# Chunk sizes, half weight loads, one evacuating engine and split stores in a depthwise-separable 1x1 convolution

## The chip, the cores and the metric

The kernel runs on one core of a Trainium2 chip. The metric is the device time of one execution in microseconds (us), as the median of several runs. Profiles are of single executions; their own time stands beside their span.

## The reference

The input is one image of 384 x 384 positions with 384 channels, in bf16. The depthwise kernel is 1 x 1, so the depthwise step only scales each channel, and the pointwise step is a matrix product over channels:

```
for i in range(k):            # k = 1
    for j in range(k):
        out = out + xp[:, i:i+H, j:j+W, :] * dw[i, j][None, None, None, :]
return jnp.einsum('bhwc,cd->bhwd', out, pw)
```

So out[n, d] = sum over c of x[n, c] * dw[c] * pw[c, d], for N = 147,456 rows n and 384 values of c and of d.

## The kernel before

**Tiling.** The rows are cut into 288 supertiles of 512 rows. Supertiles are grouped into chunks, each loaded and stored by one DMA. `_chunks` gives the sizes: 1, 1, 2, 4, then 34 chunks of 8, then 4, 2, 1, 1. Three X buffers (`NX`) hold loaded chunks and three O buffers (`NO`) hold results; two T buffers and two PSUM halves (`PS`, four banks each) alternate by supertile.

**Weights.** `load_pw` loads pw four times, once into each quarter of 32 partitions, so that four row tiles of TensorE can work side by side. All four loads count on one semaphore, `s_pw`. The scales dw are spread by four VectorE copies into `dwsel` (L186). Then twelve slices of `w_r` (six blocks b, two parities) are made as pw times dw: the even parity on VectorE (L197), the odd on ScalarE (L199). Each adds to `s_wr`, and TensorE waits for all twelve before its loop starts.

**One supertile.** VectorE transposes X into T in two halves of 32 x 32 blocks of 32-bit words, that is of bf16 pairs (L174); half h serves blocks 3h to 3h + 2. TensorE (L134) then does 48 matmuls: twelve groups (b, parity) of four (q), where q picks one quarter of the array and one PSUM bank. It waits for the half of T it needs (`s_t`), and, in the first group, for the PSUM half to be empty (`s_a` from ScalarE, `s_d` from VectorE). When half h of the groups is through, `s_pe` rises. Banks 0 to 2 are then copied to O by ScalarE (L215), bank 3 by VectorE (L212).

**Order.** The order is written out by hand. VectorE runs, for supertile jj: the copy of bank 3, then the two transposes for jj + 2. ScalarE runs one copy per supertile. TensorE runs a hardware loop over pairs of supertiles. At the first supertile of a chunk, VectorE and ScalarE wait until the store of three chunks ago has landed (`s_o`), because it used the same O buffer. SP issues nearly all DMAs in program order: the first loads, then for each chunk t the load of chunk t + 3, which waits until chunk t has been transposed, and the store of chunk t, which waits for the last copies of the chunk. A waiting DMA holds back all that SP would issue after it.

In what follows the supertiles, chunks and stores are numbered from 0.

Of the kernel before, what the change touches and what calls it, by code (L numbers as in the profile page):

```python
# [7 lines left out]
BF16 = mybir.dt.bfloat16  # L8
F32 = mybir.dt.float32
U32 = mybir.dt.uint32  # L10
COPY = mybir.ActivationFunctionType.Copy
# [3 lines left out]
NO = 3  # L15


def _chunks(n_super: int):

    head, tail = [1, 1, 2, 4], [4, 2, 1, 1]  # L20
    mid = n_super - sum(head) - sum(tail)
    assert mid > 0 and mid % LMAX == 0
    return head + [LMAX] * (mid // LMAX) + tail
# [3 lines left out]
def kernel(  # L27
# [11 lines left out]
    nc = tc.nc  # L39
    P = nc.NUM_PARTITIONS  # L40
    B, H, W, C = x.shape
    assert dw.shape[0] == 1 and dw.shape[1] == 1, "only k=1 depthwise supported"
    D = pw.shape[1]
    N = B * H * W
    assert C == 384 and D == 384 and N % 1024 == 0
    NB = C // 64

    xf = x.rearrange("b h w c -> (b h w) c")
    of = out.rearrange("b h w d -> (b h w) d")

    NS = N // 512
    chunks = _chunks(NS)
    NT = len(chunks)
    s0 = [sum(chunks[:t]) for t in range(NT)]

    consts = ctx.enter_context(tc.tile_pool(name="consts", bufs=1))
# [3 lines left out]
    pw_r = consts.tile([P, NB, 2, D], BF16, name="pw_r")  # L60
    w_r = consts.tile([P, NB, 2, D], BF16, name="w_r")
    dwt = consts.tile([32, NB, 2], BF16, name="dwt")
    dwsel = consts.tile([P, NB * 2], F32, name="dwsel")
    warm = consts.tile([P, 3], F32, name="warm")
    seed = consts.tile([P, 2], F32, name="seed")

    Xs = [bufp.tile([P, 4 * LMAX, C], BF16, name=f"X{i}") for i in range(NX)]
    Ts = [bufp.tile([P, NB, 256], BF16, name=f"T{i}") for i in range(2)]
    Os = [bufp.tile([P, 4 * LMAX * D], BF16, name=f"O{i}") for i in range(NO)]
    PS = [psum.tile([P, 4, 512], F32, name=f"ps{s}") for s in range(2)]  # L70
# [2 lines left out]
    s_t = [[nc.alloc_semaphore(f"s_t{i}{h}") for h in range(2)] for i in range(2)]  # L73
    s_pe = nc.alloc_semaphore("s_pe")
    s_a = [nc.alloc_semaphore(f"s_a{i}") for i in range(2)]
    s_d = [nc.alloc_semaphore(f"s_d{i}") for i in range(2)]
    s_o = [nc.alloc_semaphore(f"s_o{i}") for i in range(NO)]
    s_dw = nc.alloc_semaphore("s_dw")
    s_pw = nc.alloc_semaphore("s_pw")
    s_ds = nc.alloc_semaphore("s_ds")  # L80
    s_wr = nc.alloc_semaphore("s_wr")
    s_seed = nc.alloc_semaphore("s_seed")

    with tc.tile_critical():  # L84
        pw_v = pw.rearrange("(b w r) d -> w b (r d)", w=32, r=2)
        dw_v = dw.rearrange("a e (b w r) -> w (a e b) r", w=32, r=2)

        def load_pw(eng, q):
            eng.dma_start(pw_r[32 * q : 32 * q + 32].rearrange("w b r d -> w b (r d)"), pw_v).then_inc(s_pw, 16)  # L89

        def load_x(t):
            L = chunks[t]
            r = 512 * s0[t]
            src = xf[r : r + 512 * L, :].rearrange("(p s) c -> p (s c)", p=P)
            d = nc.sync.dma_start(Xs[t % NX][:, : 4 * L, :].rearrange("p s c -> p (s c)"), src)  # L95
            if t >= NX:
                je = s0[t - NX] + chunks[t - NX] - 1
                d._wait_ge(s_t[je % 2][1], je // 2 + 1)
            d.then_inc(s_x[t % NX], 16)

        def store(t):
            L = chunks[t]
            r = 512 * s0[t]
            je = s0[t] + L - 1
            nc.sync.wait_ge(s_d[je % 2], je // 2 + 2)
            dst = of[r : r + 512 * L, :].rearrange("(q p j) d -> p q (j d)", q=4, p=P)
            d = nc.sync.dma_start(dst, Os[t % NO][:, : 4 * L * D].rearrange("p (q e) -> p q e", q=4))  # L107
            d._wait_ge(s_a[je % 2], je // 2 + 2)
            d.then_inc(s_o[t % NO], 16)


        nc.scalar.dma_start(dwt[:], dw_v).then_inc(s_dw, 16)
        load_x(0)
        load_pw(nc.scalar, 2)
        load_pw(nc.sync, 0)
        load_pw(nc.scalar, 3)
        load_pw(nc.sync, 1)
        for t in range(1, NX):
            load_x(t)
        for t in range(NT):  # L120
            if t + NX < NT:
                load_x(t + NX)
            store(t)
        for o in range(NO):
            nc.sync.wait_ge(s_o[o], 16 * len(range(o, NT, NO)))


        def supertile(s, rv):
            for b in range(NB):
                for par in range(2):  # L130
                    for q in range(4):
                        if par == 0 and q == 0 and b in (0, 3):
                            nc.tensor.wait_ge(s_t[s][b // 3], rv)
                        mm = nc.tensor.matmul(  # L134
                            PS[s][:, q, :D],
                            lhsT=Ts[s][32 * q : 32 * q + 32, b, par::2],
                            rhs=w_r[32 * q : 32 * q + 32, b, par, :],
                            start=(b == 0 and par == 0),
                            stop=(b == NB - 1 and par == 1),
                            tile_position=(32 * q, 0),  # L140
                        )
                        if b == 0 and par == 0 and q == 0:
                            mm._wait_ge(s_a[s], rv)
                        elif b == 0 and par == 0 and q == 3:
                            mm._wait_ge(s_d[s], rv)
                        if b in (2, 5) and par == 1 and q == 3:
                            mm.then_inc(s_pe)

        nc.tensor.wait_ge(s_wr, 2 * NB)
        with nc.tensor.Fori(0, NS // 2, 1) as it:  # L150
            rv = nc.tensor.to_reg(it + 1)
            for s in range(2):
                supertile(s, rv)


        for s in range(2):
            nc.vector.memset(seed[:, s : s + 1], 0.0).then_inc(s_d[s])  # L157
        nc.gpsimd.memset(warm[:], 0.0).then_inc(s_seed)  # L158
        for s in range(2):
            c = nc.scalar.copy(warm[:, s + 1 : s + 2], warm[:, 0:1])  # L160
            if s == 0:
                c._wait_ge(s_seed, 1)
            c.then_inc(s_a[s])

        def transposes(t, j):
            jj = s0[t] + j
            L = chunks[t]
            s = jj % 2
            Xw = Xs[t % NX][:].bitcast(U32)[:, : 4 * L, :].rearrange("p (k l) c -> p k l c", l=L)
            Tw = Ts[s][:].bitcast(U32).rearrange("p b (i k) -> p b k i", k=4)  # L170
            for h in range(2):
                if h == 0 and j == 0:
                    nc.vector.wait_ge(s_x[t % NX], 16 * (t // NX + 1))  # L173
                ins = nc.vector.transpose(  # L174
                    out=Tw[:, 3 * h : 3 * h + 3],
                    in_=Xw[:, :, j, 96 * h : 96 * h + 96].rearrange("p k (b w) -> p b k w", w=32),
                )
                if jj >= 2:
                    ins._wait_ge(s_pe, 2 * (jj - 2) + h + 1)
                ins.then_inc(s_t[s][h])  # L180

        order = [(t, j) for t in range(NT) for j in range(chunks[t])]

        nc.vector.wait_ge(s_dw, 16)
        for q in range(4):
            nc.vector.tensor_copy(  # L186
                dwsel[32 * q : 32 * q + 32, :], dwt[:].rearrange("w b r -> w (b r)")
            ).then_inc(s_ds)
        transposes(*order[0])
        for b in range(NB):  # L190
            for r in range(2):
                eng = nc.vector if r == 0 else nc.scalar
                if b == 0:
                    eng.wait_ge(s_pw, 64)  # L194
                sc = dwsel[:, 2 * b + r : 2 * b + r + 1]
                if r == 0:
                    i = nc.vector.tensor_scalar_mul(w_r[:, b, r, :], pw_r[:, b, r, :], sc)  # L197
                else:
                    i = nc.scalar.activation(w_r[:, b, r, :], pw_r[:, b, r, :], COPY, scale=sc)  # L199
                if b == 0:  # L200
                    i._wait_ge(s_ds, 4)
                i.then_inc(s_wr)
        transposes(*order[1])

        for jj, (t, j) in enumerate(order):
            L = chunks[t]
            s = jj % 2
            Ov = Os[t % NO][:, : 4 * L * D].rearrange("p (q j d) -> p q j d", q=4, d=D)
            if j == 0 and t >= NO:
                nc.vector.wait_ge(s_o[t % NO], 16 * (t // NO))  # L210
                nc.scalar.wait_ge(s_o[t % NO], 16 * (t // NO))  # L211
            e = nc.vector.tensor_copy(Ov[:, 3, j, :], PS[s][:, 3, :D])  # L212
            e._wait_ge(s_pe, 2 * jj + 2)
            e.then_inc(s_d[s])
            a = nc.scalar.copy(Ov[:, 0:3, j, :], PS[s][:, 0:3, :D])  # L215
            a._wait_ge(s_pe, 2 * jj + 2)
            a.then_inc(s_a[s])
            if jj + 2 < NS:
                transposes(*order[jj + 2])


# [28 lines left out]
```

## Time and profile before

| | |
|---|---|
| median of 9 runs | 586.66 us (585.78 to 589.11) |
| profiled execution | 586.6 us |
| its span | 584.8 us |
| TensorE matmul busy | 564.2 us (96%) |
| VectorE busy | 563.9 us (96%) |
| ScalarE busy | 327.0 us (56%) |
| moved by DMA | 227.79 MB, 390 GB/s over the span |

Busy time is the sum of the stretches in which an engine was at work. A matmul's busy time covers its wait in the pipeline, so a busy TensorE is not in itself a TensorE at its peak: the distance from one supertile's end to the next tells its pace. The chain that ended last is followed back from the end of the program, at each step to what released it; its entries are read as start, length, and what ran.

### The profile page before, as it was taken

The numbers are of one execution on the slowest core, as the hardware profiler recorded it, in microseconds if no ns is written. First come the engines' busy times: TensorE is split into PE (matmuls) and PEld (weight loads), VectorE is DVE, ScalarE is ACT, GpSimd is POOL, SyncE is SP. The second block draws the span as 40 slices with busy tenths as digits, with TensorE's granted clock in tenths as the row PEclk, the third lists the DMA queues.
The fourth block names the chain that finished last, engine by engine and source line by source line (L and its number), as shares of the span: only waits on it lengthen the run. The fifth ranks groups of instructions, "written<-read, shape, count | busy, mean of one in ns | idle before, by whom it ended". The sixth has DMA issues, their size and how long they took to land.

```text
span 584.8 us, 29852 instructions
## 1 busy us (share of the span) xinstructions
PE 564.2 (96%) x13824; PEld 421.2 (72%) x13824; DVE 563.9 (96%) x876; ACT 327.0 (56%) x297; POOL 0.3 (0%) x5
## 2 busy tenths in 40 slices
PE   0999999999999999999999999999999999999995
PEld 0667777777777777777777777777777777777773
DVE  3889999999999999999999999999999999999995
ACT  3455555555555555555555555555555555555553
POOL 0000000000000000000000000000000000000000
PEclk9999999999999999999999999999999999999998
DMA  8699999999999999999999999999999999999758
GB/s 288 248 416 418 428 427 410 407 405 398 403 401 396 401 414 387 414 400 390 411 390 414 416 405 403 400 400 414 394 398 414 388 403 399 394 424 406 321 225 309
DMA packets 29277, 227.79 MB, mean 390 GB/s; under 512 B 1616, under 2 KB 5456, under 8 KB 24656
## 3 DMA queue, kind: packets, MB, share of 16 engines
q1 hardware_dynamic: 28640, 227.09, 96.9%
q10 hardware_dynamic: 624, 0.59, 0.4%
q14 instruction: 12, 0.10, 0.0%
q8 instruction: 1, 0.02, 0.0%
HBM read 114.43 MB, written 113.25 MB: 389 GB/s over the span
## 4 chain that ended last, share of the span: by engine, by line
PE 93%; DMA 5%; ACT 1%; SPq 0%; issue 0%; DVE 0%; ACTq 0%; DVEq 0%
PE ps L134 93%; DMA X<-in_x_dram 2%; DMA pw_r<-in_pw_dram 1%; DMA out_dram<-O 1%; ACT O L215 1%; ACT w_r L199 1%; DVE T L174 0%; SPq L89 0%; SPq L107 0%; SPq L95 0%; SPq L245 0%; DVEq L173 0%; ACTq L211 0%; ACTq L194 0%; SPq L84 0%
## 5 line engine op out<-in xcount | busy, mean ns | idle before, releaser
L134 PE MATMUL ps<-w_r,T 32*128 32x384 bf16 x13824 | 564.2, 322 | 14.4 <-ACT w_r L199 13.2
L134 PEld LDWEIGHTS ps<-w_r,T 32*128 32x128 bf16 x13824 | 421.2, 93 | 157.0 <-issue 15.0
L215 ACT CAST O<-ps 128x1152 bf16<-128x1152 f32 x288 | 322.3, 1119 | 245.6 <-PE ps L134 243.7
L174 DVE STREAM_TRANSPOSE T<-X 128x384 uint32<-128x384 uint32 x576 | 448.5, 854 | 1.9 <-DMA X<-in_x_dram 1.8
L212 DVE CAST O<-ps 128x384 bf16<-128x384 f32 x288 | 160.8, 558 | 7.0 <-PE ps L134 4.8
L199 ACT ACTIVATE w_r<-pw_r,dwsel 128x384 bf16<-128x384 bf16 x6 | 3.1, 601 | 5.8 <-DMA pw_r<-in_pw_dram 5.8
L186 DVE CAST dwsel<-dwt 32x12 f32<-32x12 bf16 x4 | 0.7, 164 | 3.8 <-DMA dwt<-in_dw_dram 3.7
L197 DVE TENSOR_SCALAR w_r<-pw_r,dwsel 128x384 bf16<-128x384 bf16 x6 | 1.5, 316 | 2.6 <-DMA pw_r<-in_pw_dram 2.6
L160 ACT ACT_TABLE_LOAD x1 | 1.3, 1283 | 2.3 <-issue 2.3
L157 DVE MEMSET seed<- 128x1 f32 x2 | 0.1, 59 | 1.0 <-SPq L84 1.0
L160 ACT COPY warm<-warm 128x1 f32<-128x1 f32 x2 | 0.3, 189 | 0.0
L234 POOL MEMSET const-bfloat16-1.0<- 128x1 bf16 x1 | 0.1, 103 | 0.0
L234 POOL MEMSET const-uint8-127<- 128x1 uint8 x1 | 0.1, 103 | 0.0
L158 POOL MEMSET warm<- 128x3 f32 x1 | 0.1, 101 | 0.5 <-SPq L84 0.5
L234 POOL MEMSET const-float32-0.0<- 128x1 f32 x1 | 0.1, 100 | 0.2 <-issue 0.2
L234 POOL MEMSET const-float32-1.0<- 128x1 f32 x1 | 0.1, 100 | 0.0
## 6 DMA issues: line engine op xcount, KB each, us to landing
X<-in_x_dram SPq DMA_DIRECT2D x34, 3072.0 KB, 18.0
out_dram<-O SPq DMA_DIRECT2D x34, 3072.0 KB, 22.9
X<-in_x_dram SPq DMA_DIRECT2D x2, 1536.0 KB, 12.6
out_dram<-O SPq DMA_DIRECT2D x2, 1536.0 KB, 13.6
X<-in_x_dram SPq DMA_DIRECT2D x4, 384.0 KB, 5.7
X<-in_x_dram SPq DMA_DIRECT2D x2, 768.0 KB, 10.3
out_dram<-O SPq DMA_DIRECT2D x4, 384.0 KB, 4.1
out_dram<-O SPq DMA_DIRECT2D x2, 768.0 KB, 11.4
```

The source lines that it names most:

```text
L134: mm = nc.tensor.matmul(PS[s][:, q, :D], lhsT=Ts[s][32 * q : 32 * q + 32, b, par::2], rhs=w_r[32 * q : 32 * q + 32, b, par, :], start=(b = ...
L157: nc.vector.memset(seed[:, s : s + 1], 0.0).then_inc(s_d[s])
L158: nc.gpsimd.memset(warm[:], 0.0).then_inc(s_seed)
L160: c = nc.scalar.copy(warm[:, s + 1 : s + 2], warm[:, 0:1])
L174: ins = nc.vector.transpose(out=Tw[:, 3 * h : 3 * h + 3], in_=Xw[:, :, j, 96 * h : 96 * h + 96].rearrange("p k (b w) -> p b k w", w=32),)
L186: nc.vector.tensor_copy(dwsel[32 * q : 32 * q + 32, :], dwt[:].rearrange("w b r -> w (b r)")).then_inc(s_ds)
L197: i = nc.vector.tensor_scalar_mul(w_r[:, b, r, :], pw_r[:, b, r, :], sc)
L199: i = nc.scalar.activation(w_r[:, b, r, :], pw_r[:, b, r, :], COPY, scale=sc)
L212: e = nc.vector.tensor_copy(Ov[:, 3, j, :], PS[s][:, 3, :D])
L215: a = nc.scalar.copy(Ov[:, 0:3, j, :], PS[s][:, 0:3, :D])
L234: nc = _bacc.Bacc("TRN2", target_bir_lowering=False, num_devices=1)
```

## The change

- `_chunks` gives 1, 1, 2, 2, 3, 3, 4, then 32 chunks of 8, then 6, 4, 3, 2, 1: 44 chunks instead of 42.
- Each quarter of pw is loaded in two halves of three blocks (`h`), with one semaphore for each half; the first halves are issued ahead of the second halves on both queues.
- `dwsel` is made by ScalarE. Nine of the twelve `w_r` slices are made by VectorE, and three by ScalarE (the odd parity of blocks 0, 2 and 4). TensorE waits, inside its loop, for each slice at the group that uses it, in every even supertile.
- Fourteen matmuls on a zeroed tile run ahead of TensorE's loop.
- ScalarE copies all four PSUM banks of a supertile. Only for the last supertile do VectorE (banks 2 and 3) and ScalarE (banks 0 and 1) share, and there each half has its own store, one from SP and one from ScalarE's queue. `s_d` is gone from the loop.
- The stores of chunks 22, 24, 26 and 28 are issued as two DMAs each, cut by partitions at 120, 104, 56 and 88, with a semaphore for each part.

```diff
-    head, tail = [1, 1, 2, 4], [4, 2, 1, 1]
+    head, tail = [1, 1, 2, 2, 3, 3, 4], [6, 4, 3, 2, 1]
...
-        def load_pw(eng, q):
-            eng.dma_start(pw_r[32 * q : 32 * q + 32].rearrange("w b r d -> w b (r d)"), pw_v).then_inc(s_pw, 16)
+        def load_pw(eng, q, h):
+            bs = slice(3 * h, 3 * h + 3)
+            eng.dma_start(
+                pw_r[32 * q : 32 * q + 32, bs].rearrange("w b r d -> w b (r d)"), pw_v[:, bs]
+            ).then_inc(s_pw[h], 16)
...
+        split = {NT // 2: 120, NT // 2 + 2: 104, NT // 2 + 4: 56, NT // 2 + 6: 88}
+        s_cut = {t: [nc.alloc_semaphore(f"s_cut{t}_{i}") for i in range(2)] for t in split}
...
-            nc.sync.wait_ge(s_d[je % 2], je // 2 + 2)
...
+            nc.sync.wait_ge(s_a[je % 2], je // 2 + 2)
+            if t in split:
+                c = split[t]
+                nc.sync.dma_start(dst[:c], src[:c]).then_inc(s_cut[t][0], 16)
+                nc.sync.dma_start(dst[c:], src[c:]).then_inc(s_cut[t][1], 16)
+            else:
+                nc.sync.dma_start(dst, src).then_inc(s_o[t % NO], 16)
...
-        load_pw(nc.scalar, 2)
-        load_pw(nc.sync, 0)
-        load_pw(nc.scalar, 3)
-        load_pw(nc.sync, 1)
+        for h in range(2):
+            for q in range(2):
+                load_pw(nc.scalar, 2 + q, h)
+                load_pw(nc.sync, q, h)
...
+        nc.sync.dma_start(of_last[:, 2:4], o_last[:, 2:4])._wait_ge(s_d, 1).then_inc(
+            s_last, 16
+        )
...
+        wr_eng = {(b, r): int(r == 1 and b % 2 == 0) for b in range(NB) for r in range(2)}
...
-                        elif b == 0 and par == 0 and q == 3:
-                            mm._wait_ge(s_d[s], rv)
+                        elif s == 0 and q == 0:
+                            mm._wait_ge(*wr_done[b, par])
...
-        nc.tensor.wait_ge(s_wr, 2 * NB)
+        nc.tensor.wait_ge(s_zero, 1)
+        for i in range(14):
+            nc.tensor.matmul(
+                PS[1][:, i % 4, :D],
+                lhsT=zero[32 * (i % 4) : 32 * (i % 4) + 32, 0:P],
...
+        nc.tensor.wait_ge(*wr_done[0, 0])
...
-        nc.vector.wait_ge(s_dw, 16)
+        nc.scalar.wait_ge(s_dw, 16)
         for q in range(4):
-            nc.vector.tensor_copy(
-                dwsel[32 * q : 32 * q + 32, :], dwt[:].rearrange("w b r -> w (b r)")
-            ).then_inc(s_ds)
+            nc.scalar.copy(dwsel[32 * q : 32 * q + 32, :], dwt[:].rearrange("w b r -> w (b r)")).then_inc(s_ds)
...
+            nq = 4
+            if jj + 1 == NS:
+                nq = 2
...
+                e = nc.vector.tensor_copy(Ov[:, nq:4, j, :], PS[s][:, nq:4, :D])
+                e._wait_ge(s_pe, 2 * jj + 2)
+                e.then_inc(s_d)
+            a = nc.scalar.copy(Ov[:, 0:nq, j, :], PS[s][:, 0:nq, :D])
...
+        nc.scalar.dma_start(of_last[:, 0:2], o_last[:, 0:2])._wait_ge(s_a[(NS - 1) % 2], (NS - 1) // 2 + 2).then_inc(
+            s_last, 16
+        )
```

## The prediction

> **What bounds the kernel now.** I read the busy line first, then the chain that ended last in order of time, then the steady stretch, then the landings of the transfers.
>
> ```profile
> PE 564.2 (96%) x13824; PEld 421.2 (72%) x13824; DVE 563.9 (96%) x876; ACT 327.0 (56%) x297; POOL 0.3 (0%) x5
> ...
> L174 DVE STREAM_TRANSPOSE T<-X 128x384 uint32<-128x384 uint32 x576 | 448.5, 854 | 1.9 <-DMA X<-in_x_dram 1.8
> L212 DVE CAST O<-ps 128x384 bf16<-128x384 f32 x288 | 160.8, 558 | 7.0 <-PE ps L134 4.8
> L199 ACT ACTIVATE w_r<-pw_r,dwsel 128x384 bf16<-128x384 bf16 x6 | 3.1, 601 | 5.8 <-DMA pw_r<-in_pw_dram 5.8
> ```
>
> TensorE and VectorE are both busy 96%; ScalarE has room. The chain says which counts:
>
> ```profile
> 1.88 7.73 DMA pw_r<-in_pw_dram
> ...
> 9.71 3.15 ACT w_r L199 x6
> 12.86 0.32 issue
> 13.18 4.05 PE ps L134 x48
> ...
> 18.84 12.34 DMA X<-in_x_dram
> ...
> 32.28 538.41 PE ps L134 x13248
> ...
> 571.86 7.68 DMA out_dram<-O
> ...
> 579.61 1.12 ACT O L215
> ```
>
> The end is set by one long TensorE stretch with a slow start (13.18 us of no matmul, then 4.05 us for one supertile), an X load at 31 us and a store at 579 us. The steady stretch, as the timeline shows it:
>
> ```profile
> 40.31 1.12 ACT L215 CAST O<-ps 128x1152 bf16<-128x1152 f32 x1 [0.83 <-PE ps L134]
> 40.31 0.56 DVE L212 CAST O<-ps 128x384 bf16<-128x384 f32 x1
> 40.79 1.56 DVE L174 STREAM_TRANSPOSE T<-X 128x384 uint32<-128x384 uint32 x2
> 42.26 1.12 ACT L215 CAST O<-ps 128x1152 bf16<-128x1152 f32 x1 [0.83 <-PE ps L134]
> ```
>
> One supertile takes 1.95 us. The single records show its twelve groups of four matmuls starting 162.5 ns apart (41.704, 41.866, 42.029, 42.191), and 12 x 162.5 ns is 1.95: TensorE has no gap. So the steady stretch, 286 x 1.95 = 557.7 us, can't be shortened by this change. What can is the ends and the one stall. VectorE's cast (0.48 us until the next instruction starts) and two transposes also fill about 1.95 us, but T is ready: the wait for its first half ends at 41.69, 0.18 us ahead of the group that uses it.
>
> Last, the transfers, by the tiles' own answers (O, then X):
>
> ```profile
> DMA to landing us min/median/max: 2.7/21.9/25.4
> ...
> DMA to landing us min/median/max: 4.1/16.7/20.0
> ```
>
> A store has about 32 us before its buffer is wanted again (17 supertiles less the evacuation), a load about 31. Neither is late in mid-stream. But of the sixteen increments of a store's semaphore the last comes later and later: 0.8 us behind the median at 41 us, 8.0 at 314, 9.6 at 502; the fifteenth stays 2 to 3 us behind. One DMA engine lags.
>
> [...] the first supertile took 4.05 us, the second 2.19 (17.25 to 19.44), then 1.95. [...] the trace shows one slow engine, not its number.
>
> **The change part by part.** E0, E1, ... are the ends of supertiles.
>
> *Half weight loads, per-slice waits.* Before, everything waits for four whole quarters (9.62), then for six ScalarE slices (3.15), then 0.32 for loop entry: 13.18. The landings of the four quarters were 6.45, 7.10, 8.66 and 9.62. The two first halves carry the bytes of the first two quarters, so half 0 is in at about 7.2 and half 1 at about 9.8 (eight issues instead of four: four of 0.46 us on each of SP and ScalarE, done by 3.3, ahead of the data). Dwsel moves from VectorE to ScalarE behind the later table load: four small copies from 4.9, at most 0.2 us each, done by 5.7; hidden under the weight load. VectorE transposes supertile 0 at 5.15 to 6.7, then makes four slices at 0.245 us (six took 1.47). Slice (0,0) is done at 7.6, loop entry 0.32, first matmul 7.9. Cold groups take 4.05/12 = 0.34 us, slower than VectorE makes slices, so six groups end at 9.9. Half 1 arrives at 9.8, its first slice is done at 10.15, six more cold groups give E0 = 12.2 (17.25 before): **-5.0 us**. VectorE's nine slices end at 11.1 and T1's first half follows at 11.9, just in time, so E1 is 2.1 to 2.2 later, as before. [...] The fourteen zero matmuls run near 2 us for about 1.3 us (four rounds of 0.34)[...]: 0, at best -0.6.
>
> *Chunk sizes.* Before, chunk 4 (eight supertiles) is issued at 18.84 behind store 0 and lands at 31.18; E7 to E8 is 31.14 to 34.46, so 3.32 - 1.95 = 1.37 us of stall. After, I queued every load and store in SP's order at 400 GB/s (the stretch from 20 to 52 us moved that on average). Load 4 (1.18 MB): issued at 14.2, lands at 19.3, wanted at 21.3. Loads 5 and 6: 4 us early. Load 7 (the first with eight): issued at 25, behind 9.4 MB counted from 13.8, lands at 38.5, wanted at 40.7. Stores 0 to 5 land at least 2 us before their buffers are wanted. **-1.4 us**, with some 2 us in hand.
>
> *ScalarE alone.* The evacuation grows from 1152 to 1536 elements[...]. It fits in 1.95; the bank is wanted again 1.95 us after it fills, so 0.5 us of slack stays where 0.83 was. VectorE loses the 0.48 and T comes earlier. Stores are issued 0.3 us later, loads 1 us earlier. 0 us; without this slack each 0.1 us past 1.95 would cost 29 us.
>
> *Per-slice waits in the loop.* Eleven new waits in each even supertile, 144 x 11 = 1,584, all satisfied after the first pass; the two waits for VectorE's seed semaphore go. The trace has no wait of just this kind at every group, so bounds: 0, as the existing waits at three places show (the groups at 41.866 and before keep the 162.5 ns), up to 51 ns, the length of TensorE's stand-alone semaphore instruction at 41.69. I take 0: they sit on weight loads queued ahead, and ScalarE's release comes 0.5 us ahead of its group. No gain is possible, the array being full.
>
> *Split stores* (chunks 22, 24, 26, 28). [...] 120+8 partitions use 15 and 8 engines, then 13 and 12, 14 and 12, 11 and 10. [...] One row of an eight-chunk is 4 x 6144 B at 234 ns, 0.94 us[...]; a normal engine's store lands about 15.6 us after issue[...]. Four extra issues of 0.4 us on SP, with 12 us waits to hide them. 0 us[...].
>
> *Tail.* Stores of 6, 4, 3, 2 start 4 us earlier than 4, 2, 1 for the same bytes. The last chunk's buffer waits for chunk 40's store, issued 10 us before the last matmul ends and done 5 us before: the 1.05 us wait (578.56 to 579.61) goes. The last evacuation is shared: VectorE's two banks, at twice its pace of 0.48 or twice its 0.56, take 0.96 to 1.12 us in place of 1.12; I take the pace. The two last stores move the same bytes from two queues. From the issue at 580.81 to the end of the span took 4.01: 0.96 + 0.07 + 4.01 = 5.0 against 6.26. **-1.2 us**.
>
> Sum: -5.0 - 1.4 - 1.2 = -7.6. The profiled run took 586.6 with span 584.8; so 579.0, span 577.2. The median of nine is 586.66, 0.06 off: 579.0.
>
> **Rivals.** (a) *Loads late in the new head.* For: loads 4 and 7 have only 2 us in hand, and the 1.5 KB and 768 B packets run below 400 GB/s. At 340 GB/s load 7 comes 2 to 3 us late; one TensorE stall, 581.5. Against: the measured stretch held 400 with the same kinds of packets. (b) [...] A store of 24.6 us plus 8.4 is 33 against 32; ScalarE waits in mid-stream once or twice, 1 to 2.5 us: 581. [...] (c) *Slower: the satisfied waits show.* In TensorE's stream each visible nanosecond costs 1.6 us; from 4.8 ns each they eat the whole gain; the full 51 ns gives 579 + 81 = 660. Against: the existing waits, one of them in mid-supertile, show none. (d) *Half loads don't split the landing*: both halves arrive near 9.8 because the two queues interleave; first matmul 10.5, E0 14.6: 581.4.
>
> **How the numbers follow.** Main case 0.66, (a) 0.12, (b) 0.08, (d) 0.05, (c) 0.06, something unseen 0.03. The main case runs from 577.8 (clock warm early, a shorter last landing) to 580.3 ([...] load 7 half a microsecond late). (a), (b) and (d) lie at 580 to 583. 577.5 to 582.5 holds over 8 in 10. Faster than 0.2% (1.2 us, about what nine runs between 585.78 and 589.11 can tell): all but (c) and part of the unseen, 0.92; same 0.02; slower 0.06.
>
> **What would show it.** Right: first looped matmul near 7.9 and E0 near 12.2; 1.95 us between evacuations of about 1.44 us; no TensorE wait on X near 31; evacuations without a wait on O at the end; last issue to end 4 us. Wrong: groups of matmuls further apart than 162.5 ns in even supertiles only (c); a VectorE wait on X between 20 and 42 us (a); a ScalarE wait on O near 350 to 430 us (b); the two weight semaphores filling together (d).

## The result and the profile after

The changed kernel is slower: 593.24 us median against 586.57, ratio 1.0119 (95% interval 1.0099 to 1.0139). Its runs also spread more, from 589 to 598 us, where those of before lie within 3.5. One more run, at 606 us, counts as slow and is left out of the ratio. The profiled execution took 597.5 us with a span of 595.7, so it shows the loss some 4 us larger than the median does. The forecast was 579.0.

The busy line and the evacuation's group on the page of the changed kernel:

```profile
PE 570.3 (96%) x13838; PEld 337.0 (57%) x13838; DVE 507.0 (85%) x586; ACT 417.7 (70%) x298; POOL 0.5 (0%) x6
...
L259 ACT CAST O<-ps 128x1536 bf16<-128x1536 f32 x288 | 413.6, 1437 | 167.5 <-PE ps L162 152.0
```

VectorE went from 96% to 85%, ScalarE from 56% to 70%, and one evacuation takes 1.437 us, where about 1.44 was forecast. With 1.119 us for 1,152 elements before, each of the 384 added ones costs 0.83 ns. None of this sets the time. The chain that ended last, in order of time (start, length, what):

```profile
1.89 5.20 DMA pw_r<-in_pw_dram
...
7.85 377.52 PE ps L162 x7581
...
385.39 1.45 ACT O L259
...
386.86 0.32 SPq L118
...
387.22 47.11 DMA out_dram<-O
...
434.42 1.45 ACT O L259
...
435.92 154.50 PE ps L162 x3478
...
590.44 0.96 DVE O L256
```

The start is as forecast: first matmul at 7.85 us instead of 13.18, and no load of X in the chain. Then there is an entry that the chain of before does not have: a store, issued at 387.22, that takes 47.11 us to land. L118 and L119 issue the two parts of a cut store, and this is the second part of the last one, that of chunk 28. The waits (engine, line, for whom, us in total, times, longest) say who was held:

```profile
ACT O L259 <- DMA out_dram<-O: 15.5, 2, 11.2
PEld ps L162 <- ACT O L259: 14.4, 2, 10.6
PE ps L162 <- ACT O L259: 13.7, 2, 10.2
```

ScalarE waits twice for an O buffer, and TensorE for ScalarE. The timeline has the places:

```profile
386.86 0.32 SPq L118 DMA_DIRECT2D out_dram<-O  x1
387.22 11.20 SPq L119 DMA_DIRECT2D out_dram<-O  x1
391.17 2.78 ACT L259 CAST O<-ps 128x1536 bf16<-128x1536 f32 x2 [4.34 <-DMA out_dram<-O]
...
434.42 2.78 ACT L259 CAST O<-ps 128x1536 bf16<-128x1536 f32 x2 [11.15 <-DMA out_dram<-O]
```

At 391 the wait is for chunk 26's cut store, whose last increment came at 391.1, 35 us after its issue; at 434 for chunk 28's. The distances between evacuations exceed 1.95 us by 3.83 + 1.41 around the first wait and by 10.64 + 1.68 + 0.29 around the second, 17.85 in all. Nowhere else do they, apart from the first supertile. So the 597.5 us of this execution are the forecast's 579.0 and these 17.85 us, within 0.7.

The stretches from 290 to 441 us, all engines (us, busy and count of each engine, clock, DMA share, GB/s):

```profile
290.00:385.40 95.40, 95.40 (x2356) 56.57 (x2352) 85.96 (x99) 70.36 (x50) 0.00 (x0) 1.00 0.98 372
385.40:441.00 55.60, 41.93 (x936) 23.90 (x932) 34.18 (x39) 28.15 (x20) 0.00 (x0) 0.88 0.93 348
```

In the first stretch TensorE still runs without a gap, but the DMA engines, 98% busy, move only 372 GB/s. They are busy and slow. What they leave undone here (a debt, in what follows) is paid for in the second stretch, where TensorE is busy for only 41.93 of 55.60 us.

### The profile page after: what moved, and what is told of

Same layout as the page of the kernel before. It is cut to its first block, busy times and chain, and to the rows that moved or that the text cites. A ratio compares the mean times of both kernels' runs of the same rounds, so it can differ in the third digit from the quotient of the medians.

```text
span 595.7 us, 29678 instructions
## 1 busy us (share of the span) xinstructions
PE 570.3 (96%) x13838; PEld 337.0 (57%) x13838; DVE 507.0 (85%) x586; ACT 417.7 (70%) x298; POOL 0.5 (0%) x6
## 4 chain that ended last, share of the span: by engine, by line
PE 89%; DMA 9%; ACT 0%; DVE 0%; SPq 0%; issue 0%; ACTq 0%; DVEq 0%
PE ps L162 89%; DMA out_dram<-O 8%; DMA pw_r<-in_pw_dram 1%; ACT O L259 0%; DVE O L256 0%; DVE w_r L233 0%; SPq L92 0%; SPq L100 0%; SPq L118 0%; ACTq L249 0%; SPq L292 0%; DVEq L230 0%; SPq L86 0%
## 5 line engine op out<-in xcount | busy, mean ns | idle before, releaser
L212 DVE STREAM_TRANSPOSE T<-X 128x384 uint32<-128x384 uint32 x576 | 503.8, 878 | 79.6 <-PE ps L162 18.8
L259 ACT CAST O<-ps 128x1536 bf16<-128x1536 f32 x288 | 413.6, 1437 | 167.5 <-PE ps L162 152.0
L162 PEld LDWEIGHTS ps<-w_r,T 32*128 32x128 bf16 x13824 | 336.6, 93 | 251.4 <-ACT O L259 14.4
L235 ACT ACTIVATE w_r<-pw_r,dwsel 128x384 bf16<-128x384 bf16 x3 | 1.7, 610 | 2.6 <-DMA pw_r<-in_pw_dram 2.6
L180 PE MATMUL ps<-zero 32*128 32x384 bf16 x14 | 1.5, 515 | 1.3 <-POOL zero L196 1.3
## 6 DMA issues: line engine op xcount, KB each, us to landing
X<-in_x_dram SPq DMA_DIRECT2D x32, 3072.0 KB, 18.2
X<-in_x_dram SPq DMA_DIRECT2D x2, 1536.0 KB, 13.1
out_dram<-O SPq DMA_DIRECT2D x1, 2880.0 KB, 22.1
```

Of the source, the lines that this page charges most:

```text
L162: mm = nc.tensor.matmul(PS[s][:, q, :D], lhsT=Ts[s][32 * q : 32 * q + 32, b, par::2], rhs=w_r[32 * q : 32 * q + 32, b, par, :], start=(b = ...
L180: nc.tensor.matmul(PS[1][:, i % 4, :D], lhsT=zero[32 * (i % 4) : 32 * (i % 4) + 32, 0:P], rhs=zero[32 * (i % 4) : 32 * (i % 4) + 32, :], s ...
L212: ins = nc.vector.transpose(out=Tw[:, 3 * h : 3 * h + 3], in_=Xw[:, :, j, 96 * h : 96 * h + 96].rearrange("p k (b w) -> p b k w", w=32),)
L259: a = nc.scalar.copy(Ov[:, 0:nq, j, :], PS[s][:, 0:nq, :D])
```

## The experiments

Times that come with a ratio and its interval are medians of four or five executions; all other runs below are single executions. The kernel before took 586.1 to 586.4 us beside them.

**Is it the cuts?** The first run has every store whole, all else as changed.

```diff
-        split = {NT // 2: 120, NT // 2 + 2: 104, NT // 2 + 4: 56, NT // 2 + 6: 88}
+        split = {}
```

> The changed kernel with every store whole (no cut by partitions), all else as changed. If the four cut stores cause both mid-stream waits of ScalarE (whatever the mechanism), the 17.9 us between 385 and 441 us go and the time is near 579 to 580, about 1.2% under the kernel before. If the waits come from another part (ScalarE alone, a later issue of stores), they stay and the time is 590 or more.

Measured: 579.1 us, ratio to before 0.9871 (0.9854 to 0.9889). The two stretches and the stores' landings, of this run:

```profile
290.00:385.40 95.40, 95.40 (x2356) 56.87 (x2348) 85.64 (x99) 70.36 (x50) 0.00 (x0) 1.00 1.01 402
385.40:441.00 55.60, 55.60 (x1380) 33.22 (x1372) 49.93 (x58) 41.15 (x29) 0.00 (x0) 1.00 1.00 401
```

```profile
DMA to landing us min/median/max: 2.7/21.7/23.2
```

402 GB/s instead of 372, no gap, and no store later than 23.2 us. The four cuts alone turn a gain of 7.3 us into a loss. The other way round, the kernel before with only the cuts (at the same supertiles, VectorE and ScalarE both waiting for both parts):

```diff
+            if t in split:
+                c = split[t]
+                nc.sync.dma_start(dst[:c], src[:c]).then_inc(s_cut[t][0], 16)
+                nc.sync.dma_start(dst[c:], src[c:]).then_inc(s_cut[t][1], 16)
```

> The kernel before with only the four cut stores (120, 104, 56, 88 partitions) on the same supertiles. If the cuts alone are to blame: 15 to 18 us slower than before, 600 to 606, with waits on O near 390 and 430 us, of VectorE and ScalarE. If they need ScalarE alone or the later issue of the stores to hurt: within 3 us of before.

Measured: 603.78 us beside 586.36, 17.4 us slower. Its waits:

```profile
ACT O L232 <- DMA out_dram<-O: 18.3, 3, 12.7
DVE O L229 <- DMA out_dram<-O: 16.8, 3, 11.8
```

The cuts need none of the other parts to do harm. (This is one execution, but 17 us is far outside the spread of either kernel without cuts.)

**What about the cuts?** Three things may set a cut store apart from a whole one. There are two DMAs (the two-DMAs theory of the texts below). The rows, one for each partition, may fall unevenly on the engines (the rows theory): in the changed kernel's trace the parts of 120, 8, 104, 24, 56, 72, 88 and 40 partitions came in with 15, 8, 13, 12, 14, 12, 11 and 10 single increments, whole stores with 16. And a part is not the whole 128 partitions, which may slow its packets (the ports theory). With one engine for each increment and equal shares of rows, an engine that is in all eight parts carries 8 + 1 + 8 + 2 + 4 + 6 + 8 + 4 = 41 rows, nine more than the 32 of four whole stores. This is an estimate from the increments; no trace numbers the engines. One run cuts each store by the quarter q, so that both parts have all 128 partitions; one cuts at 64, so that the parts are equal.

```diff
-                nc.sync.dma_start(dst[:c], src[:c]).then_inc(s_cut[t][0], 16)
-                nc.sync.dma_start(dst[c:], src[c:]).then_inc(s_cut[t][1], 16)
+                nc.sync.dma_start(dst[:, :2], src[:, :2]).then_inc(s_cut[t][0], 16)
+                nc.sync.dma_start(dst[:, 2:], src[:, 2:]).then_inc(s_cut[t][1], 16)
```

> The changed kernel with the same four stores issued as two DMAs, each over all 128 partitions, cut by the quarter q instead (0, 1 and 2, 3). Rows theory and ports theory: as without cuts, 579 to 581, all packets at 234 ns. Two-DMAs theory (more issues or more DMAs in flight cost): waits of ScalarE at the chunks after the cuts, 585 to 598.

```diff
-        split = {NT // 2: 120, NT // 2 + 2: 104, NT // 2 + 4: 56, NT // 2 + 6: 88}
+        split = {NT // 2: 64, NT // 2 + 2: 64, NT // 2 + 4: 64, NT // 2 + 6: 64}
```

> The changed kernel with the four stores cut at 64 partitions[...]. Rows theory[...]: no mid-stream wait, 579 to 581. Ports theory[...]: many 6144 B packets at about 470 ns, stores landing over 32 us after issue, 585 to 598. Two-DMAs theory: 585 to 598 too.

Measured: 578.86 us by quarters, 578.93 us at 64. Two DMAs instead of one cost nothing here. The cut at 64 is the more telling. From 290 to 440 us, 405 of its 4,671 packets of 6,144 B took over 400 ns, more than half of them 472 to 475, twice the usual 234; with cuts by quarters it was 1, with whole stores none, and in the changed kernel 567 of 4,424. So cutting by partitions did slow packets down, even where the parts are equal, as the ports theory said. But its time was not what that theory expected: the stores land later and still in time.

```profile
DMA to landing us min/median/max: 2.9/22.3/29.7
```

29.7 us is under the 32 us after which a buffer is wanted. Nor did the lost throughput count by itself. In the first of the two stretches this run moves 376 GB/s, hardly more than the changed kernel's 372, and TensorE has no gap in either:

```profile
290.00:385.40 95.40, 95.40 (x2356) 70.66 (x2352) 85.87 (x98) 70.36 (x50) 0.00 (x0) 1.00 1.00 376
385.40:441.00 55.60, 55.60 (x1376) 41.19 (x1372) 50.05 (x58) 40.78 (x30) 0.00 (x0) 1.00 1.01 416
```

Slow packets alone did not stop the kernel. The last of the sixteen increments trailed the first by 16.5 us at 385 us and by 11.5 at 504, so this delay was in part worked off. The traces do not number the engines, so whether the slow packets fell on the engine that lags from the start stays open.

**The dose.** Only the first cut, and only the last:

```diff
-        split = {NT // 2: 120, NT // 2 + 2: 104, NT // 2 + 4: 56, NT // 2 + 6: 88}
+        split = {NT // 2: 120}
```

> The changed kernel with only the first cut (120 and 8 partitions, 15 and 8 engines). [...] with packets at twice the time the store takes some 8 us more. Landing 28 to 31 us after issue, below 32: no wait, 579 to 580.

```diff
-        split = {NT // 2: 120, NT // 2 + 2: 104, NT // 2 + 4: 56, NT // 2 + 6: 88}
+        split = {NT // 2 + 6: 88}
```

> The changed kernel with only the last cut (88 and 40 partitions, 11 and 10 engines). [...] rows theory, 3.7 us more, landing near 28, no wait, 579 to 580. Rows and slow packets together: [...] 7 to 15 us more, landing 30 to 38 us after issue, a wait of 0 to 6 us, 579 to 585.

Measured: 578.58 us for the first alone (119 slow packets), 585.27 us for the last alone (189 such packets). The last one's loss was about the largest expected of rows and slow packets together, but not at the place. No wait follows the cut; they come 170 us later, among the small chunks of the tail:

```profile
563.55 2.78 ACT L259 CAST O<-ps 128x1536 bf16<-128x1536 f32 x2 [1.88 <-DMA out_dram<-O]
...
565.38 2.97 DVE L212 STREAM_TRANSPOSE T<-X 128x384 uint32<-128x384 uint32 x4 [2.32 <-DMA X<-in_x_dram]
...
571.64 2.78 ACT L259 CAST O<-ps 128x1536 bf16<-128x1536 f32 x2 [2.97 <-DMA out_dram<-O]
```

The debt was still there: the last increment trailed the first by 15.0 us at 430 us and by 17.0 at 552.

**Extra bytes without SBUF.** To load some engines more than the others, but with no partition involved, this run keeps the stores whole and issues, beside those four stores, copies from HBM to a scratch tensor with an outer dimension of 8.

```diff
+            if t in extra:
+                k = extra[t]
+                xs = xf[: 256 * k, :].rearrange("(g r) c -> g (r c)", g=8)
...
+                nc.sync.dma_start(scratch[:, : 12288 * k], xs).then_inc(s_ex, 16)
```

> The changed kernel with whole stores, and beside the stores of chunks 22, 24, 26 and 28 a copy from HBM to a scratch tensor in HBM whose outer dimension is 8[...], without touching SBUF. This adds work that the reference does not have. Rows theory: the same harm as the cuts, 590 or more. If extra bytes alone are the 8.4 us of the sum: landing of the slowest up to 24 to 33 us, wait 0 to 2.5 us, 579 to 581.5.

Measured: 589.17 us, 10.1 above the run with whole stores, with one packet of 6,144 B over 400 ns. In one point the run is not what its text says. The first three copies came in with 8 single increments each, as meant; the fourth, whose target is the whole scratch tensor, came in with 16. With one engine for each increment it was spread over all 16. If the first three went to the same eight, these carried some 172 KB of copies each (24.6 + 49 + 49 + 49) and the other eight 49, where an engine that is in all eight parts of the cuts has, by the estimate above, some 221 KB more than with whole stores (nine rows of 24.6). The waits of ScalarE:

```profile
ACT O L269 <- DMA out_dram<-O: 13.2, 9, 3.1
```

Nine waits, each of at most 3.1 us, the first at 464 us, where the last copy was issued at 387. So this run has a loss, but not the two long waits of the changed kernel at 391 and 434 us: by the distances between evacuations some 2.4 us fall between 463 and 532 us, and some 7.5 from 563 us on, among the small chunks. The sixteen increments of each semaphore show why. At 291 us the last came 9.0 us after the first, the fifteenth 2.3. At 431 us the last is 18.2 us behind, at 478 us 20.0; the fifteenth never exceeds 4.8. With whole stores and no copies the last is 9.7 behind at 478. Read with one engine for each increment, all engines but one caught up; that one, by its lag of 9.0 us at 291 us the one that lagged from the start, did not. The copies' own packets show it too: of the 8, 8 and 16 packets of 49,152 B in the second, third and fourth copy, one each took 2.08 or 2.09 us and every other 1.82. Copies of as many bytes dealt to all 16 engines were not run beside this one. The same copies with an outer dimension of 7 ask whether the slow engine stays out when seven engines carry them, so that its lag stays, or is among the seven, so that it grows again:

```diff
-                xs = xf[: 256 * k, :].rearrange("(g r) c -> g (r c)", g=8)
+                xs = xf[: 224 * k, :].rearrange("(g r) c -> g (r c)", g=7)
```

> As the run with copies on 8 engines, but with an outer dimension of 7[...] (same bytes per engine; added work that the reference does not have). [...] its lag stays at 8 to 10 us, no wait on O, 579 to 580. [...] lag up to 20 us and 587 to 591 again, as with 8.

Measured: 589.86 us, and the last increment 18.7 us behind at 478 us. The fourth copy came in with 16 single increments here too, but the second and third, with seven packets of 49,152 B each, tell: six took 1.82 us and one 2.08 or 2.09. So the slow engine was among the seven as it was among the eight; which one it is was not shown. This run was made on another chip than the one with 8, and the lag is much the same on both (18.7 and 20.0 us).

**Would more buffers help?** With the cuts kept, a fourth O buffer gives each store 15.6 us more.

```diff
-NO = 3
+NO = 4
```

> The changed kernel, cuts kept, with four O buffers instead of three: a store's buffer is wanted 15.6 us later, some 47.5 us after issue instead of 32. If the waits come only from stores that land too late for their buffer (35.5 and 47.1 us in the changed kernel's trace), they shrink to at most 1 us: 579 to 581, with the slow 6144 B packets still there. If late X loads or the blocked issue on SP (11.2 us at 387 us) matter by themselves, a wait on X or a later store takes their place: 585 or more.

Measured: 592.54 us, against 593.24 with three. The waits changed their name:

```profile
DVE T L212 <- DMA X<-in_x_dram: 18.6, 6, 6.4
...
PE ps L162 <- DVE T L212: 7.5, 3, 4.4
```

ScalarE no longer waits for O, but VectorE waits for X (18.6 us, against 7.1 in the changed kernel): loads are late too, and one took 37.5 us to land. By the distances between evacuations 6.1 us are lost near 431 us, where the changed kernel lost 17.85 in mid-stream, and some 7.7 from 572 us on, in the tail. That a late store is the whole matter is refuted. The fourth buffer only changed who waited, and when.

**Do the other parts bring what they were said to?** Whole stores, and the weights or the chunk sizes of before:

```diff
-        wr_eng = {(b, r): int(r == 1 and b % 2 == 0) for b in range(NB) for r in range(2)}
+        wr_eng = {(b, r): int(r == 1) for b in range(NB) for r in range(2)}
...
-                        elif s == 0 and q == 0:
-                            mm._wait_ge(*wr_done[b, par])
...
-        nc.tensor.wait_ge(*wr_done[0, 0])
+        for e in range(2):
+            nc.tensor.wait_ge(s_wr[e], NB)
```

> The changed kernel with whole stores and the weights as before: four whole loads, six slices each on VectorE and ScalarE, and one wait for all ahead of TensorE's loop, with no waits for slices inside it. If the half loads and slice waits bring 5 us and cost nothing in the loop: 584 to 585 with first matmul near 13.2. If the waits in the loop cost something, the loss is smaller than 5 us and supertiles are closer than 1.95 us apart.

```diff
-    head, tail = [1, 1, 2, 2, 3, 3, 4], [6, 4, 3, 2, 1]
+    head, tail = [1, 1, 2, 4], [4, 2, 1, 1]
```

> The changed kernel with whole stores and the chunk sizes of before. By the sum: a wait on X of 1 to 1.5 us near 26 us comes back, and at the end a wait for the 4-chunk's store of about 1 us: 581 to 582. If the sizes don't matter, 579.

Measured: 584.66 us with the old weights (ratio to before 0.9967, 0.9952 to 0.9982), 5.6 above 579.1, and 582.73 us with the old chunks (0.9932, 0.9914 to 0.9950), 3.6 above. With the old weights, and so without a wait for slices in the loop, supertiles stay 1.95 us apart: those waits cost nothing that shows. With the old chunks the wait on X is back:

```profile
28.38 3.60 DVE L212 STREAM_TRANSPOSE T<-X 128x384 uint32<-128x384 uint32 x5 [4.97 <-DMA X<-in_x_dram]
```

It cost 4.3 us of TensorE here (this execution took 585.0), where 1 to 1.5 were expected: TensorE starts 5.1 us earlier than in the kernel before (8.08 against 13.18), and the load of eight supertiles lands only 2.9 us earlier (28.3 against 31.2). At the end the wait for O returned with 1.27 us.

**The zero matmuls.** Sixty-four instead of fourteen:

```diff
-        for i in range(14):
+        for i in range(64):
```

> The changed kernel with whole stores and 64 instead of 14 matmuls on the zeroed tile ahead of the loop: 16 rounds of 0.32 us from 1.3 to at most 6.4 us[...]. If matmuls on zeros raise the clock: the first supertiles run at 1.95 us pace as soon as their slices are there, E0 near 11.4 and E1 near 13.6, 1 us gained: 577.8 to 578.3. If zeros don't count: 579 as with 14.

Measured: 578.83 us (578.5 to 579.5), ratio 0.9873 (0.9857 to 0.9890): not told apart from 579.1. The timeline shows that TensorE was at full pace in time:

```profile
7.91 1.16 PE L162 MATMUL ps<-w_r,T 32*128 32x384 bf16 x24 [1.31 <-DVE w_r L233]
...
9.76 1.29 PE L162 MATMUL ps<-w_r,T 32*128 32x384 bf16 x24 [0.69 <-DVE w_r L233]
...
11.10 1.44 ACT L259 CAST O<-ps 128x1536 bf16<-128x1536 f32 x1 [1.10 <-PE ps L162]
```

The first 24 matmuls take 1.16 us (2.11 us with fourteen), but the second half of the weights and then T1 come no sooner, so E0 gains 0.9 us and E1 (13.72) 0.6. The fastest versions tried are thus the changed kernel with whole stores, with either number of zero matmuls: some 1.3% faster than before, 2.4% faster than the changed kernel.

## Why the prediction was wrong

**The split stores, put at 0 us, were the step that failed; the rest of the sum held.** Without them the sum's 579.0 stands beside 579.1, and the span's 577.2 beside 577.3. The terms hold one by one, so this is not luck:

- *Half weight loads, -5.0.* First matmul 7.85 (7.9 forecast), E0 11.99 (12.2); with whole stores E1 is at 14.32, 5.1 us earlier than before (19.44), and 5.6 us lost when it was taken back. E0 to E1 took 2.90 in the changed kernel's profile and 2.28 with whole stores, where 2.1 to 2.2 were forecast. The first record of a granted clock of 1.00 stands at 13.73 us in the one and at 12.52 in the other; in the changed kernel groups of four matmuls started 0.32 us apart before it and 0.1625 after. E1 came at most 0.6 us later than forecast.
- *Chunk sizes, -1.4.* No matmul waited on X in the head with whole stores. Taking the sizes back cost more than the sum gave them, since a faster start makes the old sizes worse.
- *ScalarE alone, 0, and waits in the loop, 0.* Every supertile of the run with whole stores is 1.95 us after the last, from the second on. Rival (c), the only one that ended on the slower side, did not happen.
- *Tail, -1.2.* From the last matmul's end to the end of the span 5.28 us (572.02 to 577.3) against 5.0.
- *Rival (d)*: the first halves let VectorE start at 7.20, the second at 9.46; they do split.

The step on the cuts put 8.4 us over 110 us, part of it worked off on the way, against a normal engine with 16 us in hand. The 8.4 us are nine rows of 0.94 us, the estimate above for an engine that is in all eight parts; that any engine is was not shown. Three terms were wrong.

1. *The duration of a packet.* I priced the cut stores with the 234 ns of whole ones. In the changed kernel the 6,144 B packets from 290 to 440 us averaged 273 ns, 10.9 us over the 234 for each of the sixteen engines (0.6 before the cuts), and the parts came in with 8 to 15 single increments, not 16. With the 8.4 us of rows that is, by this estimate, some 19 us on an engine that is in all parts, more than twice what I allowed.
2. *The recovery.* In the run with 8 all increments but the last made it up: the fifteenth never came more than 4.8 us after the first. The last hardly did. In the kernel before, with nothing added, its lag on the stores still grew, from 8.5 us at 306 us to 10.7 at 511. In the run with 8 engines it rose from 9.0 to 20.0 us and was still 18.9 at 556, long after the last copy had landed (417). In the changed kernel the last increment recovered a little: 16.4 us behind at 481 us, 13.1 at 540.
3. *The engine that counts.* A store has landed when the last of its increments has come: 24.6 us of 32 in the kernel before and 22.1 in the changed kernel just ahead of the cuts, not 15.6. Rival (b) reckoned with the 24.6 and named the place, the waits on O, but priced them at "once or twice, 1 to 2.5 us" and gave it 0.08. Extra copies alone cost 10 us; the debt that was not worked off was charged at chunk after chunk, or in the tail.

The four cuts together cost 14.1 us between medians and 18.4 between the two profiled executions. Part of that is not transfer at all: after each wait TensorE restarted at a granted clock of 0.50, from 392.66 to 396.0 us and from 435.92 to 440.4 (hence the mean of 0.88 above), about 1.4 us lost after the first and 2.0 after the second. The four extra issues on SP, priced at 0.4 us each, took 0.33 to 0.64 us except the last, 11.20. With four O buffers that one took 1.26 us and the kernel lost as much, so it is not what cost the time.

How far slow packets and uneven rows each carry the whole is not settled: extra copies, three of the four on eight engines, cost 10, and at other places; slow packets in equal parts cost nothing; the four cuts cost 14 to 18. No run had unequal parts of a store without slow packets. Why a packet takes twice as long is not shown either, only that 405 did with cuts at 64 partitions and 1 with cuts by quarters.

## What to carry to other kernels

When the DMA engines are busy 96% of the time, as here, cost a transfer in the time of the slowest engine, not in bytes or GB/s: read how far the last of a semaphore's increments trails the others, and how that distance grows. What was added to that engine was hardly worked off here, so a harmless-looking edit in mid-stream was paid at the next tight buffer or in the tail, and another buffer only moved the wait. If a store has to be cut, cut it along a free dimension, so that all 128 partitions stay in each part: that cost nothing here (578.86 us, against 579.1 with whole stores), and gained nothing.

## What the runs showed of the hardware

- Of the sixteen increments of each part of a cut store, those counted above (15, 8, 13, 12, 14, 12, 11 and 10) came in one by one and the remainder at once. With an outer dimension of 8 three copies came in with 8 single increments each; the fourth, whose target was the whole scratch tensor, came in with 16, and so it did with an outer dimension of 7.
- The lag of the last increment is read as that of one engine, which the traces do not number: of the packets of 49,152 B in each of the second, third and fourth copies with an outer dimension of 8, one took 2.08 or 2.09 us and every other 1.82.
- An issue on SP took 11.20 us at 387 us, where the three other issues at L119 took 0.33 to 0.64. In the kernel before with cuts the last such issue took 10.41 us.
- Matmuls on zeros raised TensorE's clock: with 64 of them from 1.29 us the first record of a granted clock of 1.00 stands at 6.88, before the first real one at 7.91, and the first 24 real ones took 1.16 us. With fourteen it stands at 12.52, some 5 us after the first real one, and they took 2.11.
